# A 2-D spectral filter with backward pass: chunked complex column transform, and a twice-folded real one through DRAM

## The chip, the cores and the metric

The kernel runs on one core of one Trainium2 chip. Time is in device microseconds (us) of that core for one launch; lower is better. Times are medians of several runs; one execution was also taken with the hardware profiler. The engines are TensorE (PE, with its weight loads PEld), VectorE (DVE), ScalarE (ACT), GpSimd (POOL) and SyncE (SP). SP and POOL issue nearly all DMAs here.

## The reference

Two branches are mixed by a gate, and the kernel computes the output and all gradients. Branch A is a 2-D real Fourier transform of x (2048 x 1024), a product with a complex weight W (2048 x 513), and the transform back; branch B is a dense layer with squared relu and hidden width F = 3584.

```python
def _A_ref(x, w_r, w_i):
    X = rfft2(x.astype(float32), axes=(-2, -1))
    X = X * (w_r + 1j * w_i)
    return irfft2(X, s=(S, D), axes=(-2, -1)).astype(bfloat16)

def _B_ref(x, w1, b1, w2, b2):
    h = einsum("bsd,df->bsf", x, w1) + b1
    r = where(h > 0, h, 0)
    return einsum("bsf,fd->bsd", r * r, w2) + b2

g = sigmoid((x * gate_w).sum(-1, keepdims=True))
a = _A_ref(x, A_w_r, A_w_i)
b = _B_ref(x, B_w1, B_b1, B_w2, B_b2)
out = g * a + (1 - g) * b
```

Both branches work on x. The nine outputs are out, the gradients of x, w_r and w_i, of w1, b1, w2, b2 and of gate_w. The backward pass of branch A is the same transform on g times the incoming gradient, a product with the conjugate of W, and a transform back; the gradient of W is the product of the one spectrum with the conjugate of the other.

## The kernel before

Rows are taken as 16 tiles of 128; tile t holds the rows p*16 + t. P is 128, S = 2048, D = 1024, Df = 513.

*Loading (L266 to L293).* Each of the 16 tiles of x and of the incoming gradient is loaded, alternately by SP and POOL (`dma`, L186, takes the two queues in turn), transposed by TensorE in eight 128 x 128 blocks into xT and goT, and the gate sums are formed.

*Chunks (from L416).* The 520 padded columns of the half spectrum are cut in nine chunks of 64 (the last of 8). For each, `f1_stage` (matmul L325) multiplies the rows by cosine and sine matrices; `fwd_chain` (L348 to L377) does the transform over the 2048 rows as 128 times 16, both complex: matmuls with `amat`, transposes, matmuls with `kmat`. W is loaded by columns and transposed too (L467). `cmul` (L490 to L502) forms the three complex products, shared between DVE and POOL: the filtered spectrum `ybuf`, the backward one `dxb`, and the gradient of W, which goes to DRAM as gWc_scr. `inv_c_t` (L391 to L407) applies the 16-point stage backwards and transposes into the large buffer RT.

*Loops back.* `t_loop` (L540 to L590) runs over 16 tiles: matmuls with `apmat`, eight or nine transposes (L568), matmuls with the inverse row matrix g5 (L578), a scaled copy to `abf`, and a store to a_scr. The nine chunks of `dxb` come back from dX_scr through `inv_c_t` into the same RT, and `t_loop` runs again and stores to gx_scr. In the first run a dot product with the incoming gradient is formed (L590).

*Dense part.* goT is scaled by 1 - g (L621 to L626). Four row blocks of 512 rows (L677 to L806) run forward and backward through the dense layer and write out and gx. Then seven groups of hidden units (L849 to L868) give the gradients of w1 and w2: each has 128 matmuls at L858 from go and h2l, and 128 at L866 from dhl and x. In the third group the gradient of W is gathered from gWc_scr into `gall` by nine POOL DMAs (L849) and written to the outputs by two (L851, L852).

The order on each engine is the program's order; tiles with a tag share a ring of `bufs` buffers, and a DMA or operation that writes a tile waits until the last user of that buffer is done.

Of the kernel before, what the change touches and what calls it, by code (L numbers as in the profile page):

```python
# [10 lines left out]
P = 128  # L11
# [10 lines left out]
class Geo:  # L22

    def __init__(self, S, D, F, CC=64):
# [4 lines left out]
        self.L_LO = P // self.S2  # L29
        self.Df = D // 2 + 1  # L30
        self.NLH = -(-self.Df // self.L_LO)
        self.NCOLC = self.NLH * self.L_LO
        self.CC = CC
        assert CC % self.L_LO == 0
        self.CH = CC // self.L_LO
        self.chunks = []
        lh = 0
        while lh < self.NLH:
            n = min(self.CH, self.NLH - lh)
            self.chunks.append((lh, n))  # L40
            lh += n
        self.NJ = len(self.chunks)
        self.zbase = []
        b = 0
        for (lh0, n) in self.chunks:
            self.zbase.append(b)
            b += 2 * n * self.L_LO
        self.ZC = b
        self.NBZ = -(-self.ZC // P)
# [12 lines left out]

    def ccj(self, j):
        return self.chunks[j][1] * self.L_LO


def build_consts(g: Geo):
    S, D, S2, L_LO = g.S, g.D, g.S2, g.L_LO
    two_pi = 2.0 * np.pi
    c = {}  # L70
    c["identb"] = np.eye(P, dtype=np.float32).astype(ml_dtypes.bfloat16)
    c["ident16"] = np.eye(P, dtype=np.float32).astype(FDT_NP)
    CDS = np.zeros((g.NJ, P, g.DC, 2 * g.CC), dtype=np.float64)
    d = np.arange(D)
    for j, (lh0, n) in enumerate(g.chunks):
        CCj = n * L_LO
        ls = np.arange(lh0 * L_LO, lh0 * L_LO + CCj)
        ang = two_pi * ((ls[None, :] * d[:, None]) % D) / D
        cr = np.cos(ang)
        ci = -np.sin(ang)  # L80
        valid = (ls < g.Df)[None, :]
        cr = np.where(valid, cr, 0.0)
        ci = np.where(valid, ci, 0.0)
        ci[:, (ls % (D // 2)) == 0] = 0.0
        blk = np.concatenate([cr, ci], axis=1)
        CDS[j, :, :, : 2 * CCj] = blk.reshape(g.DC, P, 2 * CCj).transpose(1, 0, 2)
    c["cds"] = CDS.astype(np.float32).astype(ml_dtypes.bfloat16)
    pp = np.arange(P)[:, None]
    ff = np.arange(P)[None, :]
    A = np.zeros((P, S2, 3, P))  # L90
    Ap = np.zeros((P, S2, 3, P))
    for t in range(S2):
        m = (ff * (S2 * pp + t)) % S
        th = two_pi * m / S
        A[:, t, 0, :] = np.cos(th)
        A[:, t, 1, :] = -np.sin(th)
        A[:, t, 2, :] = np.sin(th)
        m2 = (pp * (S2 * ff + t)) % S
        ph = two_pi * m2 / S
        Ap[:, t, 0, :] = np.cos(ph)  # L100
        Ap[:, t, 1, :] = np.sin(ph)
        Ap[:, t, 2, :] = -np.sin(ph)
    c["amat"] = A.reshape(P, S2 * 3, P).astype(np.float32).astype(FDT_NP)
    c["apmat"] = Ap.reshape(P, S2 * 3, P).astype(np.float32).astype(FDT_NP)
    pt = np.arange(P) // L_LO
    pa = np.arange(P) % L_LO
    delta = (pa[:, None] == pa[None, :]).astype(np.float64)
    ang = two_pi * ((pt[:, None] * pt[None, :]) % S2) / S2
    K = np.zeros((P, 3, P))
    K[:, 0, :] = np.cos(ang) * delta  # L110
    K[:, 1, :] = -np.sin(ang) * delta
    K[:, 2, :] = np.sin(ang) * delta
    c["kmat"] = K.astype(np.float32).astype(FDT_NP)
    G = np.zeros((g.NBZ * P, D))
    for j, (lh0, n) in enumerate(g.chunks):
        CCj = n * L_LO
        ls = np.arange(lh0 * L_LO, lh0 * L_LO + CCj)
        ang = two_pi * ((ls[:, None] * d[None, :]) % D) / D
        coef = np.where((ls == 0) | (ls == D // 2), 1.0, 2.0)[:, None]
        valid = (ls < g.Df)[:, None]  # L120
        gr = np.where(valid, coef * np.cos(ang), 0.0)
        gi = np.where(valid, -coef * np.sin(ang), 0.0)
        gi[(ls % (D // 2)) == 0, :] = 0.0
        b = g.zbase[j]
        G[b : b + CCj] = gr
        G[b + CCj : b + 2 * CCj] = gi
    c["g5"] = G.reshape(g.NBZ, P, D).transpose(1, 0, 2).astype(np.float32).astype(FDT_NP)
    return c

# [14 lines left out]
def kernel(  # L144
# [30 lines left out]
    S2, L_LO, DC, DW, DCH, FC = g.S2, g.L_LO, g.DC, g.DW, g.DCH, g.FC  # L175
    CH, CC, NJ = g.CH, g.CC, g.NJ
# [6 lines left out]
    dmat_rr = _RR([nc.scalar])  # L183
# [4 lines left out]
    def dma_t(out, in_):  # L188
        return dmat_rr().dma_start_transpose(out=out, in_=in_)

    w_rv = A_w_r.rearrange("(k2 k1) l -> k1 k2 l", k1=P)
    w_iv = A_w_i.rearrange("(k2 k1) l -> k1 k2 l", k1=P)
    o2v = out_2.rearrange("(k2 k1) l -> k1 k2 l", k1=P)
    o3v = out_3.rearrange("(k2 k1) l -> k1 k2 l", k1=P)
# [10 lines left out]
    ident16 = pers.tile([P, P], FDT, name="ident16", tag="ident16")  # L205
    dma(ident16[:], cten["ident16"].ap())
    kmat = pers.tile([P, 3, P], FDT, name="kmat", tag="kmat")
    dma(kmat[:], cten["kmat"].ap())

# [8 lines left out]
    omg = pers.tile([P, S2], FP32, name="omg", tag="omg")  # L218
    gpg = pers.tile([P, S2], FP32, name="gpg", tag="gpg")
    rsx = pers.tile([P, S2], FP32, name="rsx", tag="rsx")  # L220
    rsgo = pers.tile([P, S2], FP32, name="rsgo", tag="rsgo")
# [8 lines left out]
    ones_f = pers.tile([P, 1], FP32, name="ones_f", tag="ones_f")  # L230
    nc.vector.memset(ones_f[:], 1.0)
    b2row = pers.tile([1, D], BF16, name="b2row", tag="b2row")
    dma(b2row[:], B_b2.rearrange("(o d) -> o d", o=1))
    dcval = pers.tile([1, 1], FP32, name="dcval", tag="dcval")
# [8 lines left out]
    a_scr = dram.tile([S2, P, D], BF16, name="a_scr")  # L243
    gx_scr = dram.tile([S2, P, D], BF16, name="gx_scr")
    dX_scr = dram.tile([NJ, P, 2 * CH * P], FDT, name="dX_scr")
    SC = S // P
    gWc_scr = dram.tile([NJ, P, 2, S2, CC], BF16, name="gWc_scr")
# [5 lines left out]
    with tc.tile_pool(name="p0sb", bufs=3) as p0, tc.tile_pool(  # L253
        name="p0ps", bufs=2, space=bass.MemoryType.PSUM
    ) as p0ps, tc.tile_pool(name="p0small", bufs=2) as p0s:
        sgate = p0s.tile([P, S2], FP32, name="sgate", tag="sgate", bufs=1)
        for which in range(2):
            src = x_perm if which == 0 else go_perm
            dstT = xT if which == 0 else goT
            for t in range(S2):  # L260
                xt = p0.tile([P, D], BF16, name="xt", tag="xt", bufs=8)
                dma(xt[:], src[t])
                junk = p0.tile([P, D], BF16, name="junk", tag="junk")
                junk2a = p0.tile([P, D], BF16, name="junk2a", tag="junk2a")
                if which == 0:
                    nc.vector.tensor_tensor_reduce(  # L266
                        out=junk[:], in0=xt[:], in1=gatew_bc[:], scale=1.0, scalar=0.0,
                        op0=ALU.mult, op1=ALU.add, accum_out=sgate[:, t : t + 1],
                    )
                    nc.scalar.activation(junk2a[:], xt[:], ACT.Copy, accum_out=rsx[:, t : t + 1])  # L270
                else:
                    nc.scalar.activation(junk2a[:], xt[:], ACT.Copy, accum_out=rsgo[:, t : t + 1])
                for dc0 in range(0, DC, 4):
                    nb = min(4, DC - dc0)
                    pt = p0ps.tile([P, 4, P], BF16, name="pt", tag="pt")
                    for i in range(nb):
                        nc.tensor.transpose(pt[:, i, :], xt[:, (dc0 + i) * P : (dc0 + i + 1) * P], identb[:])
                    nc.any.tensor_copy(out=dstT[:, dc0 : dc0 + nb, t * P : (t + 1) * P], in_=pt[:, 0:nb, :])
        nc.scalar.activation(gcol[:], sgate[:], ACT.Sigmoid)
        nc.vector.tensor_scalar(out=omg[:], in0=gcol[:], scalar1=-1.0, scalar2=1.0, op0=ALU.mult, op1=ALU.add)  # L280
        nc.vector.tensor_tensor(out=gpg[:], in0=gcol[:], in1=omg[:], op=ALU.mult)
        t1 = p0s.tile([P, 2], FP32, name="t1", tag="t1")
        nc.vector.reduce_sum(out=t1[:, 0:1], in_=rsx[:], axis=mybir.AxisListType.X)
# [644 lines left out]
```

## Time and profile before

| | us |
|---|---|
| median of three runs | 2336.31 |
| the runs | 2332.72, 2336.31, 2339.97 |
| span of the profiled execution | 2334.1 |
| loading and transposing | 0 to 75 |
| nine chunks | 75 to 465 |
| loops back | 465 to 749 |
| four row blocks | 749 to 1866 |
| weight gradients | 1866 to 2334 |

No other time of the profiled execution itself is listed than its span. The stages follow each other on TensorE, so their ends can be read from the lines of its instructions. In the views that follow, "busy" is the time in which an engine works on an instruction; "x" stands for the count; the granted clock is the share of full speed that TensorE was given in that stretch; "<-" after a number of idle microseconds names what ended the wait. A group's row has the busy time in us and the mean of one instruction in ns.

### The profile page before, as it was taken

The page shows a single profiled execution, that of the slowest core. Times are in us where ns is not written, and L with a number is a line of the kernel's source. Part 1 is how long each engine was busy: PE and PEld are TensorE (multiplying, and loading weights), DVE is VectorE, ACT ScalarE, POOL GpSimd, SP SyncE. Part 2 cuts the span into 40 slices and gives each one's busy share as a digit, 9 for nine tenths or more (in the row PEclk, how much of TensorE's full clock was granted, in tenths as well). Part 3 has the DMA queues.
Part 4 walks back from the last instruction along what each step waited for, and adds up shares of the span by engine and source line. Part 5 has one row for each costly group of instructions (what it writes and reads, how often), then busy time and mean ns, then how long its engine had stood idle before and what let it go on. Part 6 is the DMA issues. An engine that isn't in the chain of part 4 may idle for free. (4 is left out here: it accounts for less than half of the span.)

```text
span 2334.1 us, 29795 instructions
## 1 busy us (share of the span) xinstructions
PE 1920.0 (82%) x11632; PEld 965.5 (41%) x11632; DVE 555.9 (24%) x1114; ACT 723.1 (31%) x1550; POOL 558.9 (24%) x844
## 2 busy tenths in 40 slices
PE   2878878668788888888988799878977783999998
PEld 2756656523333344344433344324433231444443
DVE  4253453624323422223211222202202100000000
ACT  5756556423533343123410043103440010111111
POOL 2042232311011412242211221222121251222200
PEclk9988988679999899999999999999988987999999
DMA  5211110142212556575544455534573498333310
GB/s 156 87 38 37 51 42 24 38 119 77 74 42 74 179 189 215 176 207 164 205 138 145 125 192 191 166 120 158 165 248 124 131 259 136 112 109 112 109 39 26
DMA packets 198068, 291.61 MB, mean 125 GB/s; under 512 B 56743, under 2 KB 142661, under 8 KB 197670
## 3 DMA queue, kind: packets, MB, share of 16 engines
q0 software_dynamic: 48704, 151.04, 21.6%
q1 hardware_dynamic: 147926, 136.30, 18.8%
q10 hardware_dynamic: 1296, 2.36, 0.4%
q8 instruction: 91, 1.49, 0.3%
q14 instruction: 51, 0.42, 0.1%
HBM read 201.38 MB, written 88.23 MB: 124 GB/s over the span
## 5 line engine op out<-in xcount | busy, mean ns | idle before, releaser
L740 PE MATMUL acc<-w2c,h2T 128*128 128x512 bf16 x896 | 213.8, 393 | 48.7 <-DMA w2c<-in_B_w_dram 38.8
L704 PE MATMUL ph<-xT,w1g 128*128 128x512 bf16 x896 | 236.5, 387 | 7.2 <-DMA w1g<-in_B_w_dram 7.2
L858 PE MATMUL pw<-go,h2l 128*128 128x512 bf16 x896 | 204.9, 391 | 44.5 <-ACT wo L860 20.5
L797 PE MATMUL accg<-w1Ttc,dhT 128*128 128x512 bf16 x672 | 173.5, 398 | 58.6 <-DMA w1Ttc<-w1T_scr 49.8
L866 PE MATMUL pw<-dhl,x 128*128 128x512 bf16 x896 | 195.1, 379 | 3.9 <-ACT wo L868 3.9
L797 PEld LDWEIGHTS <-dhT 128*128 128x128 bf16 x896 | 87.1, 100 | 182.7 <-issue 106.2
L712 PE MATMUL pd<-goT,w2Tfc 128*128 128x512 bf16 x672 | 161.3, 381 | 0.2
L722 ACT COPY h2S<-ptr 128x512 bf16<-128x512 bf16 x112 | 65.6, 586 | 307.6 <-PE ptr L720 220.7
L740 PEld LDWEIGHTS <-h2T 128*128 128x128 bf16 x896 | 89.7, 101 | 168.5 <-issue 75.9
L858 PEld LDWEIGHTS <-h2l 128*128 128x128 bf16 x896 | 89.2, 100 | 159.0 <-issue 54.8
L578 PE MATMUL pa<-g,zT 128*128 128x512 f16 (+1 forms) x576 | 139.9, 381 | 0.0
L866 PEld LDWEIGHTS <-x 128*128 128x128 bf16 x896 | 87.5, 98 | 110.3 <-issue 5.0
L713 DVE SCALAR_TENSOR_TENSOR dhT<-pd,rT 128x512 bf16<-128x512 f32 x112 | 77.4, 691 | 207.9 <-PE pd L712 203.6
L860 ACT CAST wo<-pw 128x512 bf16<-128x512 f32 x56 | 32.7, 586 | 268.3 <-PE pw L858 150.5
L708 ACT ACTIVATE rT<-ph,b1col 128x512 bf16<-128x512 f32 x112 | 77.1, 688 | 124.2 <-PE ph L704 124.1
L704 PEld LDWEIGHTS <-w1g 128*128 128x128 bf16 x896 | 80.0, 99 | 66.5 <-DMA w1g<-in_B_w_dram 7.4
L878 DVE CAST r<-pb 1x512 bf16<-1x512 f32 x2 | 1.4, 678 | 444.7 <-PE pb L876 444.7
L712 PEld LDWEIGHTS <-w2Tfc 128*128 128x128 bf16 x672 | 65.8, 98 | 81.0 <-issue 3.8
L709 ACT ACTIVATE h2T<-rT 128x512 bf16<-128x512 bf16 x112 | 70.5, 629 | 90.4 <-PE acc L740 79.7
L868 ACT CAST wo<-pw 128x512 bf16<-128x512 f32 x56 | 32.8, 586 | 186.9 <-PE pw L866 135.2
L578 PEld LDWEIGHTS <-zT 128*128 128x128 f16 (+1 forms) x576 | 50.7, 97 | 87.7 <-issue 36.3
L186 POOL DMA_DIRECT2D out_dram<-wo x56 | 30.5, 545 | 228.4 <-ACT wo L860 114.7
(226 smaller groups left out, 2928.7 us busy)
## 6 DMA issues: line engine op xcount, KB each, us to landing
w1g<-in_B_w_dram SPq DMA_DIRECT2D x14, 1024.0 KB, 5.5
w1g<-in_B_w_dram POOLq DMA_DIRECT2D x14, 1024.0 KB, 6.1
w2c<-in_B_w_dram SPq DMA_DIRECT2D x28, 512.0 KB, 3.5
w2c<-in_B_w_dram POOLq DMA_DIRECT2D x28, 512.0 KB, 4.2
w2Tfc<-w2T_scr POOLq DMA_DIRECT2D x42, 256.0 KB, 3.6
w2Tfc<-w2T_scr SPq DMA_DIRECT2D x42, 256.0 KB, 2.8
w1Ttc<-w1T_scr POOLq DMA_DIRECT2D x84, 128.0 KB, 2.3
w1Ttc<-w1T_scr SPq DMA_DIRECT2D x84, 128.0 KB, 2.1
```

The costliest lines, as they stand in the source:

```text
L578: nc.tensor.matmul(pa[:, dch * DW : (dch + 1) * DW], lhsT=zT[0:w, blk, :], rhs=g5[0:w, blk, dch * DW : (dch + 1) * DW], start=(blk == 0), ...
L704: nc.tensor.matmul(ph[:], lhsT=w1g[:, dc, fcg * P : (fcg + 1) * P], rhs=xT[:, dc, cols], start=(dc == 0), stop=(dc == DC - 1))
L708: nc.scalar.activation(rT[:], ph[:], ACT.Relu, bias=b1col[:, fc : fc + 1])
L709: nc.scalar.activation(h2T[:, fc, :], rT[:], ACT.Square)
L712: nc.tensor.matmul(pd[:], lhsT=w2Tf[:, ec, :], rhs=dbT[:, ec, cols], start=(ec == 0), stop=(ec == DC - 1))
L713: nc.vector.scalar_tensor_tensor(out=dhT[:, fc, :], in0=pd[:], scalar=2.0, in1=rT[:], op0=ALU.mult, op1=ALU.mult, accum_out=gb1part[:, fc, ...
L722: nc.scalar.copy(out=stg[:, :, fcg * P : (fcg + 1) * P], in_=ptr[:])
L740: nc.tensor.matmul(accs[i][:], lhsT=h2T[:, fc, i * P : (i + 1) * P], rhs=w2c[:, r_, :], start=(fc == 0), stop=False)
L797: nc.tensor.matmul(accs[i][:], lhsT=dhT[:, fc, i * P : (i + 1) * P], rhs=w1Tt[:], start=(fc == 0), stop=(fc == FC - 1))
L858: nc.tensor.matmul(pw[:], lhsT=h2l[sc][:, fb * P : (fb + 1) * P], rhs=db_t[sc][:, ecols], start=(sc == 0), stop=(sc == SC - 1))
L866: nc.tensor.matmul(pw[:], lhsT=x_t2[sc][:, db * P : (db + 1) * P], rhs=dhl[sc][:], start=(sc == 0), stop=(sc == SC - 1))
L868: nc.any.tensor_copy(out=wo[:], in_=pw[:])
```

## The change

The transform of branch A is written anew; the dense part stays.

*Forward rows.* The complex row transform becomes a real one of half the width twice over: the row of 1024 is folded at 512 and at 256 (sum and difference of mirrored halves) on DVE, so four groups of 256 numbers remain. A real 16-point stage over the rows comes first, as eight matmuls with the data as weights and `kf` as the moving matrix, which at the same time transposes; for the second tensor `kf` is scaled by the gate. Eight matmuls with `cf` (2305 columns in all) give 1024 real numbers a row, even and odd frequencies, which are copied as u and stored to z_scr. Loading and transposing the tile for the dense part (`load_row`) is part of the same pass.

*Columns.* In eight steps m, two of the 16 column groups, m and 16 - m, are loaded from z_scr. `spectrum` unpacks them with sums and differences, and multiplies by `amat`; W and its gradient are read and written in their natural row order, so the transposes of W and of its gradient, gWc_scr and `gall` are gone. The products run on DVE; `inverse` multiplies by `apmat` and packs into y_scr.

*Back rows.* Each of 32 passes loads a row tile r, does the 16-point stage with `ki`, eight matmuls with `ci`, unfolds on DVE into yo and stores it to a_scr or gx_scr, now in f16 and unscaled. The scale YS is applied where the dense part uses them.

```diff
-            f1_stage("A", pair, [uv for (_, uv) in uA], jps, xT, None, cdsp)
-            f1_stage("B", pair, [uv for (_, uv) in uB], jps, goT, gcol, cdsp)
-            XSA, bufUA, bufTA = fwd_chain("A", j, jb, jps, bUA, uAv)
-            XSB, bufUB, bufTB = fwd_chain("B", j, jb, jps, bUB, uBv)
...
-        t_loop("B", RT, tb, tps, apmat, g5, gx_scr, False)
...
+        ps2 = fx.enter_context(tc.tile_pool(name="fps2", bufs=3, space=bass.MemoryType.PSUM))
...
+        def s1(T, i, xt, kmat):
+            uv = fb.tile([P, 2, H], FDT, name="uv", tag="uv", bufs=2)
+            nc.vector.tensor_tensor(out=uv[:, 0, :], in0=xt[:, 0:H], in1=xt[:, H:D], op=ALU.add)
+            nc.vector.tensor_tensor(out=uv[:, 1, :], in0=xt[:, 0:H], in1=xt[:, H:D], op=ALU.subtract)
...
+            nc.vector.tensor_tensor(out=f[:, 0:2, 1:Q], in0=a0, in1=a1, op=ALU.add)
+            nc.vector.tensor_tensor(out=f[:, 2:4, 1:Q], in0=a0, in1=a1, op=ALU.subtract)
...
+            for b in range(8):
+                nc.tensor.matmul(pk[:, b, :], lhsT=fl[:, b * P : (b + 1) * P], rhs=kmat, start=True, stop=True)
+            ft = fb.tile([P, 8, P], FDT, name="ft", tag="ft", bufs=2)
+            nc.scalar.copy(out=ft[:], in_=pk[:])
+            pu = ps2.tile([P, 2, H], FP32, name="pu", tag="ps2")
+            o = 0
+            for (b, bank, lo, n, st) in FWD:
+                nc.tensor.matmul(
+                    pu[:, bank, lo : lo + n], lhsT=ft[:, b, :], rhs=cf[:, o : o + n],
...
+            u = fb.tile([P, H, 2], FDT, name="u", tag="u", bufs=3)
+            nc.any.tensor_copy(out=u[:].rearrange("p j b -> p b j"), in_=pu[:])
+            dma(z_scr[T][:].rearrange("c (p i) l -> i (c p) l", i=S2)[i], u[:].rearrange("p j b -> p (j b)"))
...
+        def load_row(i, T):
+            xt = fb.tile([P, D], BF16, name=f"nat{T}", tag=f"nat{T}", bufs=2)
+            dma(xt[:], (go_perm if T else x_perm)[i])
+            pt = ps2.tile([P, DC, P], BF16, name="pt", tag="ps2")
+            for b in range(DC):
+                nc.tensor.transpose(pt[:, b, :], xt[:, b * P : (b + 1) * P], identb[:])
+            nc.scalar.copy(out=(goT if T else xT)[:, :, i * P : (i + 1) * P], in_=pt[:])
+            return xt
...
+                nc.vector.tensor_tensor(out=pm[:, 2:0:-1, :], in0=R, in1=I, op=ALU.add)
+                nc.vector.tensor_tensor(out=pm[:, 0::3, :], in0=R, in1=I, op=ALU.subtract)
...
+                mm(px[:, 0, :], lhsT=C, rhs=re, start=True, stop=False)
+                mm(px[:, 1, :], lhsT=C, rhs=im, start=True, stop=False)
...
+                mm(px[:, 0, :], lhsT=Sn, rhs=im, start=False, stop=True)
+                mm(px[:, 1, :], lhsT=N, rhs=re, start=False, stop=True)
+                (nc.scalar.copy if (j + T) % 2 == 0 else nc.vector.tensor_copy)(out=x[:, j, :, 0:H], in_=px[:])
+            nc.vector.tensor_tensor(out=x[:, :, :, 0::H], in0=sp[:], in1=sgn[:], op=ALU.mult)
...
+                (nc.scalar.copy if (j + T) % 2 == 0 else nc.vector.tensor_copy)(out=v[:, j, :, 0:H], in_=pv[:])
...
+            dma(y_scr[T][:].rearrange("c p l -> p c l")[:, m : m + 9 : 8, :], pc[:].rearrange("p j c l -> p j (c l)"))
...
+                V(out=t1_[:, :, :, 0:W1], in0=X, in1=wr, op=ALU.mult)
+                V(out=t2_[:, :, :, 0:W1], in0=X, in1=wi, op=ALU.mult)
...
+            for c_, dst_w in enumerate((out_2, out_3)):
+                nc.gpsimd.dma_start(out=rows2(dst_w, m), in_=gw[:, :, c_, 0:W1])
...
+                r = fb.tile([P, H, 2], FDT, name="r", tag="u", bufs=3)
+                nc.sync.dma_start(out=r[:].rearrange("p j b -> p (j b)"), in_=y_scr[T][:].rearrange("c (p i) l -> i (c p) l", i=S2)[i])
...
+                nc.scalar.copy(out=rt[:], in_=pk[:])
...
+                nc.scalar.copy(out=e[:], in_=pu[:])
...
+                yo = fb.tile([P, D], FDT, name="yo", tag="u", bufs=3)
...
+                dma((a_scr if T == 0 else gx_scr)[i], yo[:])
...
-                        out=ot[:], in0=a_pc[:], scalar=gcol[:, t : t + 1], in1=bsc[:], op0=ALU.mult, op1=ALU.add,
+                        out=ot[:], in0=a_pc[:], scalar=gcs[:, t : t + 1], in1=bsc[:], op0=ALU.mult, op1=ALU.add,
...
-                    nc.vector.tensor_tensor(out=gxo[:], in0=gx1[:], in1=gxf_pc[:], op=ALU.add)
+                    nc.vector.scalar_tensor_tensor(
+                        out=gxo[:], in0=gxf_pc[:], scalar=YS, in1=gx1[:], op0=ALU.mult, op1=ALU.add,
...
-            if fg == min(2, g.FG - 1):
...
-                            nc.gpsimd.dma_start(out=gall[:, :, :, j * CC : j * CC + CCj_], in_=gWc_scr[j][:, :, :, 0:CCj_])
-                    with nc.allow_non_contiguous_dma(reason="gw output rows"):
-                        nc.gpsimd.dma_start(out=o2v[:, :, :], in_=gall[:, 0, :, 0 : g.Df])
-                        nc.gpsimd.dma_start(out=o3v[:, :, :], in_=gall[:, 1, :, 0 : g.Df])
```

How the rows stand on three engines is shown below; the number behind a name tells apart the tiles of one name, each row is an instruction (line, operation, out<-in, size).

SP in the loop back of the first tensor, before: the loads for the next stage, then the stores, with no load between them.

```order
L186 DMA dX_scr_106<-dxb_4725 128x2048
L186 DMA dxl_6734<-dX_scr_106 128x2048
L186 DMA dxl_6812<-dX_scr_106 128x2048
L186 DMA a_scr_104<-abf_5865 128x1024
L186 DMA a_scr_104<-abf_5922 128x1024
```

SP in the back rows of the first tensor, now.

```order
L427 DMA r_2686<-y_scr0_100 128x1024
L427 DMA r_2722<-y_scr0_100 128x1024
L171 DMA a_scr_96<-yo_2713 128x1024
L427 DMA r_2758<-y_scr0_100 128x1024
L171 DMA a_scr_96<-yo_2749 128x1024
L427 DMA r_2794<-y_scr0_100 128x1024
L171 DMA a_scr_96<-yo_2785 128x1024
```

Loads and stores now alternate on one queue; r_2758 lies in the buffer of yo_2713, and r_2794 in that of yo_2749.

DVE in a chunk, before: products and sums of the complex multiplication with evictions of the next stage among them (POOL has other products).

```order
L490 TENSOR_TENSOR tmp2_5101<-xsb_A_4928,WS_5079 128x1024
L496 TENSOR_TENSOR ybuf_5102<-tmp1_5100,tmp2_5101 128x1024
L490 TENSOR_TENSOR tmp2_5101<-xsb_A_4928,WS_5079 128x1024
L352 CAST bufT_A_5514<-pA_5539 128x2x8
L502 TENSOR_TENSOR ybuf_5102<-tmp1_5100,tmp2_5101 128x1024
L490 TENSOR_TENSOR tmp2_5101<-xsb_B_5062,WS_5079 128x1024
L396 CAST rsb_a_5146<-pCi_5151 128x512
L496 TENSOR_TENSOR dxb_5103<-tmp1_5100,tmp2_5101 128x1024
```

DVE in a column step, now: the last two sums of the first tensor's filtered spectrum, the unpacking of the next step (pm), and then the second tensor's products.

```order
L403 TENSOR_TENSOR y_2193<-t1_2189,t2_2190 128x2x513
L404 TENSOR_TENSOR y_2193<-t1_2189,t2_2190 128x2x513
L319 TENSOR_TENSOR pm_2274<-z_2272 128x2x512
L347 TENSOR_TENSOR x1_2166<-sp_2167,k_sgn_125 128x4x2
L320 TENSOR_TENSOR pm_2274<-z_2272 128x2x512
L368 CAST v_2196<-si_2197 128x4
L399 TENSOR_TENSOR t1_2223<-x1_2166,w_2130 128x4x513
L367 CAST v_2196<-pv_2207 128x2x512
L400 TENSOR_TENSOR t2_2224<-x1_2166,w_2130 128x4x513
L371 TENSOR_TENSOR pc_2217<-v_2196 128x1024
```

A row has twice the elements, all products are here, and evictions (L367) stand between them.

ACT in the forward rows, now: of a pass the copy of the transposed tile, of the 16-point stage (ft), and of the wide matmuls (u).

```order
L272 CAST u_403<-pu_394 128x2x512
L286 COPY xT_65<-pt_408 128x8x128
L262 CAST ft_438<-pk_429 128x1024
L297 ACTIVATE gcol_69<-sgate_106 128x1
L272 CAST u_449<-pu_440 128x2x512
L286 COPY goT_66<-pt_456 128x8x128
L262 CAST ft_483<-pk_474 128x1024
```

Three copies of 1024 columns a pass all stand on ACT, and each lies between two groups of TensorE's matmuls.

More of the change, by code (lines that the diff above doesn't have):

```diff
@@ L75, in build_consts @@
[L75 to L86, printed above, removed]
@@ L114, in build_consts @@
[L114 to L126, printed above, removed]
@@ L251 @@
     dh_scr = dram.tile([g.FG, SC, P, g.FGW], BF16, name="dh_scr")
[L253 to L279, printed above, removed]
@@ L578, in t_loop @@
                     nc.tensor.matmul(
-                        pa[:, dch * DW : (dch + 1) * DW], lhsT=zT[0:w, blk, :], rhs=g5[0:w, blk, dch * DW : (dch + 1) * DW],
-                        start=(blk == 0), stop=(blk == g.NBZ - 1),
-                    )
-            abf = tb.tile([P, D], BF16, name="abf", tag="abf")
-            for dch in range(DCH):
-                nc.scalar.activation(abf[:, dch * DW : (dch + 1) * DW], pa[:, dch * DW : (dch + 1) * DW], ACT.Copy, scale=inv_sd)
-            dma(dst_scr[t], abf[:])
@@ new lines @@
+                dma((a_scr if T == 0 else gx_scr)[i], yo[:])
+                if T == 0:
+                    go_ = fb.tile([P, D], BF16, name="go_", tag="nat1", bufs=2)
+                    dma(go_[:], go_perm[i])
+                    junk = fb.tile([P, D], BF16, name="junkt", tag="f", bufs=2)
+                    nc.vector.tensor_tensor_reduce(
+                        out=junk[:], in0=yo[:], in1=go_[:], scale=YS, scalar=0.0,
+                        op0=ALU.mult, op1=ALU.add, accum_out=aGo[:, i : i + 1],
+                    )
```

624 lines of the change are left out of this document (232 added, 392 removed).

## The prediction

> **What bounds the kernel now.** I read the page's head first, then busy time by stage, the chain that ended last, and single stretches.
>
> ```profile
> span 2334.1 us, 29795 instructions
> ...
> PE 1920.0 (82%) x11632; PEld 965.5 (41%) x11632; DVE 555.9 (24%) x1114; ACT 723.1 (31%) x1550; POOL 558.9 (24%) x844
> ```
>
> TensorE (PE) works 82% of 2334.1 us. The median of the runs shown, 2336.31, lies 2.2 above this span; what lies around the span is put at that, and the sum is made in the span. By stage, with the columns length, busy us (count) of PE, weight load, DVE, ACT and POOL, granted clock, DMA share, GB/s:
>
> ```profile
> 0.00:75.00 75.00, 29.65 (x260) 23.11 (x261) 41.09 (x94) 44.00 (x80) 17.14 (x29) 0.95 0.56 160
> 75.00:465.00 390.00, 308.34 (x3285) 236.57 (x3286) 170.51 (x243) 223.14 (x665) 113.53 (x76) 0.85 0.14 40
> 465.00:749.00 284.00, 228.25 (x1257) 98.33 (x1256) 82.53 (x138) 106.52 (x238) 41.28 (x95) 0.95 0.23 71
> 749.00:1866.00 1117.00, 941.77 (x4976) 425.34 (x4974) 257.23 (x633) 283.87 (x456) 279.82 (x466) 0.96 0.54 171
> 1866.00:2334.00 468.00, 412.00 (x1857) 182.16 (x1857) 4.54 (x9) 65.53 (x112) 107.09 (x179) 0.94 0.43 113
> ```
>
> The rows are loading and transposing, the nine chunks, the loops back, the four row blocks, and the weight gradients. The first three, 749 us, are the transform: TensorE is busy 566 of them. The last two are the dense layers, which the change leaves alone but for two scalings and one gather. The chain that ended last shows that gather (start, length, what):
>
> ```profile
> 1926.33 7.76 DMA gall<-gWc_scr
> 1935.94 26.81 DMA out_dram<-wo
> 1963.43 18.32 DMA out_dram<-wo
> 1982.49 22.83 PE pw L858 x96
> 2005.33 27.63 PE pw L866 x128
> ```
>
> **The change, part by part.** *End of the transform.* The dense part's first loads stand on SP behind the last gx_scr store:
>
> ```profile
> 748.86 0.32 SPq L186 DMA_DIRECT2D gx_scr<-abf  x1
> 751.01 0.33 SPq L186 DMA_DIRECT2D w2r<-in_B_w_dram  x1
> ```
>
> So the transform ends at 751.0. I build its new end from the engine that is late in each of three stages.
>
> *Forward rows (32 passes).* Start: 4.2 MB of constants go ahead of the second row's load on SP, and the first pass waits for b1row as now.
>
> ```profile
> 8.49 0.20 PE L240 MATMUL b1ps<-identb,b1row 28*128 28x28 bf16 x1 [8.49 <-DMA b1row<-in_B_b_dram]
> amat<-c_amat SPq DMA_DIRECT2D x1, 1536.0 KB, 6.2
> xt<-in_grad_out_dram SPq DMA_DIRECT2D x8, 256.0 KB, 3.9
> ```
>
> 4.2 MB at 1536 KB per 6.2 us is 17 us; 8.7 + 17 + 3.9 = 29.6, and pass 3 reaches its wide matmuls near 31.5.
>
> A pass on TensorE is eight transposes, eight 128-column products, then eight matmuls of 2305 columns in all. Each group waits for ACT to copy the one before, and the next pass's transposes stand behind the last. So the wide matmuls and three ACT copies of 1024 columns add up, less the part where the next transposes run beside the u copy, since PSUM has three buffers.
>
> ```profile
> L573 ACT COPY zT<-pzt 128x1024 f16<-128x1024 f16 x17 | 17.2, 1012 | 4.5 <-PE pzt L568 4.5
> 603.50 0.62 PE L403 MATMUL pTi<-ident,rsb 128*128 128x128 f16 x8
> 144.94 1.04 PE L515 MATMUL pWo<-identb,gW 128*128 128x128 bf16 x8 [6.45 <-DVE gW L496]
> 600.00:620.00 20.00, 14.41 (x101) 1.00 0.28 93
> 130.00:150.00 20.00, 10.88 (x73) 0.67 0.14 40
> ```
>
> Eight 128-column matmuls took 0.62 us where the granted clock was 1.00 (fourth row) and 1.04 where it was 0.67 (fifth). Taking off 0.17 us for the tail (an estimate), a column is 0.44 or 0.85 ns, and 2305 columns 1.18 or 2.13 us. ACT gives 3 x 1.01; handovers I estimate at 0.1. A pass is 4.3 us at the full clock and 5.3 at the low one. ACT then sets the pace with TensorE in gaps of a microsecond, so I take 4.45, near the full clock. 31.5 + 28 x 4.45 + 1.2 + 1.0 = 158. DVE needs at most 3.6 us a pass and is hidden.
>
> z goes out and back through DRAM at 2.3 and 3.2 us:
>
> ```profile
> gx_scr<-abf POOLq DMA_DIRECT2D x8, 256.0 KB, 2.3
> dxl<-dX_scr SPq DMA_DIRECT2D x4, 512.0 KB, 3.2
> ```
>
> The first tensor's last row is out 4.4 us earlier, so DVE begins the columns at 160.
>
> *Columns (8 steps).* DVE does nearly all of it:
>
> ```profile
> L496 DVE TENSOR_TENSOR ybuf<-tmp,tmp 128x1024 f16<-128x1024 f16 x8 | 5.5, 692 | 0.8
> L496 DVE TENSOR_TENSOR ybuf<-tmp,tmp 128x128 f16<-128x128 f16 x1 | 0.2, 225 | 0.1
> L492 DVE SCALAR_TENSOR_TENSOR tmp<-xsb_B,xsb_A 128x1024 f16<-128x1024 f16 x32 | 37.8, 1221 | 0.5
> L766 DVE TENSOR_TENSOR dg<-aGo,dg 128x1 f32<-128x1 f32 x16 | 2.2, 156 | 0.0
> L396 DVE CAST rsb<-pCi 128x512 f16<-128x512 f32 x10 | 6.9, 688 | 30.3 <-PE pCi L392 29.9 <-PE pCi L395 0.3
> ```
>
> A two-byte tensor_tensor costs 0.521 ns an element (692 less 225 ns over 896): 1.23 us for 2052. An f32 eviction of 1024 I take as 1.22, twice the 688 less its fixed 0.15, or as the third row. Per tensor and step: two folds 1.38, eviction 1.22, edges 0.16, two products 2.46, two sums 1.39, eviction 1.22, edge 0.14, unfolding 1.38 + 0.31 = 9.67. Both tensors and the weight gradient (two products, two sums, an edge: 4.01) make 23.35 us; eight, less some 4 us in step 0, which folds nothing, make 183. The stalls where DVE waits for the inverse matmuls and ACT's eviction are shown nowhere in this form: 1.0 us a step if TensorE has the full clock, 4.6 if the low one (estimates from the column prices above). I take 3, since TensorE mostly idles here: 24, and 3 for filling. 160 + 183 + 27 = 370. Before, POOL shared the products and DVE had 171 us of work in 390.
>
> The gradient's 16 output DMAs leave from POOL, which has nothing behind them in this stage but y stores of alternate tensors; these I cost at nothing, covered by the next step's 23 us.
>
> *Back rows (32 passes).* The tile r that a row is loaded into and the tile yo that the finished row is stored from share three buffers, taken in turn: r of pass i+2 gets the buffer of yo of pass i, so its load waits until that store has landed. A period of two passes is thus a circle: DVE 1.95 (five operations at the prices above), store, load, eight products, ACT copy, wide matmuls, ACT copy.
>
> ```profile
> a_scr<-abf SPq DMA_DIRECT2D x16, 256.0 KB, 2.0
> w2Tfc<-w2T_scr SPq DMA_DIRECT2D x42, 256.0 KB, 2.8
> ```
>
> 1.95 + 2.0 + 2.8 + 0.65 + 1.04 + 1.18 + 1.04, and handovers of some 0.25: 10.9 us; 12.3 at the low clock. I take 11.6, in the middle. First row at 372; 15 periods, 174; pass 31 some 4 us behind pass 30: 550, and with DVE and store **554**, 197 us before 751.0. In the first tensor's passes a dot product also runs,
>
> ```profile
> L590 DVE CUSTOM_DVE_ANT_0 junkt<-abf,got 128x1024 bf16<-128x1024 bf16 x16 | 19.5, 1217 | 0.0
> ```
>
> hidden in the 5 us that DVE waits per pass; uncovered it costs 16 x 1.2 = 19 us.
>
> *Dense part.* The row blocks keep their work and order; loads swap between SP and POOL, which I put at nothing, from -5 to +5. Two scale factors move into operations of the same length.
>
> *Gather gone.*
>
> ```profile
> 1908.59 10.52 PE L866 MATMUL pw<-dhl,x 128*128 128x512 bf16 x48
> 1936.50 1.16 POOL L852 DMA_DIRECT2D out_dram<-gall  x1
> 1961.68 0.54 POOL L186 DMA_DIRECT2D dhl<-dh_scr  x1 [20.60 <-DMA out_dram<-gall]
> 1963.46 6.54 PE L858 MATMUL pw<-go,h2l 128*128 128x512 bf16 x16 [19.14 <-ACT wo L868]
> ```
>
> From 1908.59 to 2005.33 stand two groups of 128 matmuls that take 27.63 each in the chain: 96.7 - 55.3 = 41 us lost. POOL waits 20.60 us for the gathered output before it can issue dhl. All of it should go; I take 40, since some DMA traffic remains.
>
> Sum: 2334.1 - 197 - 40 = 2097, plus 2.2: **2099 us**.
>
> **Rivals.** (1) *TensorE stays at the low clock through the transform.* For it: TensorE idles in small gaps throughout, and the row at 0.67 has 10.88 us busy in 20. Against: the stage from 465 shows 0.95 at 80% busy. Forward rows 28 x 0.8 = 23, columns 8 x 1.6 = 13, back rows 15 x 0.7 = 11: 2146. [...]
>
> (2) *The gap at 1940 stays.* The wo stores that hold the chain may be held by the h2l and dhl loads, not by the gather: + 40, 2140. Against it speaks POOL's wait on out_dram<-gall.
>
> (3) *DVE does not halve products with W.* W is bf16, spread over two planes, against f16. No such row is in the trace; bounds are the 692 and 1221 rows. At the latter a product costs 1.06 us more: six a step, + 51; with all sums and folds at 0.53 more, fourteen a step, + 110: 2150 to 2210. [...]
>
> (4) *The shared buffers do not bind.* If loads were early enough, a back pass would cost about 3.55 us (two ACT copies, wide matmuls, handovers): 32 x 3.55 = 114 instead of 182, so 2032. Against it: three buffers, two users.
>
> (5) *Slower.* The circle's round trip through DRAM is the one cost that can grow large:
>
> ```profile
> 1866.00:1908.00 42.00, 32.54 (x127) 0.84 0.95 272
> go<-in_grad_out_dram SPq DMA_DIRECT2D x8, 256.0 KB, 12.5
> ```
>
> At a DMA share of 0.95 a load of 256 KB took 12.5 us. Store and load at that price are 25 us in place of 4.8, so 16 x 20 = 323: 2422, slower. It decides from 237 / 16 = 14.8 us more a period. But two rows out and two in per 11.6 us are only some 90 GB/s, plus go rows, far below 272.
>
> **How the numbers follow.** Forecast 0.56, (1) 0.15, (2) 0.12, (3) 0.08, (4) 0.06, (5) 0.03. The forecast's own range: all at the full clock -32, DVE and row blocks -5 to -12: 2055; upward the low clock in part and a round trip 1 us longer (+16): 2130. To (1) and (2) belongs the stretch up to 2155; outside remain (4), most of (3) and (5), under 0.2: **2045 to 2160**. A measurement of this kernel tells 0.3% from no change; (5) alone can be slower, 0.03, and its border 0.01 within 0.3%: faster 0.96.
>
> **What would show it.** Forward passes 4.3 to 4.6 us apart between wide matmuls, ending near 158; DVE busy over 85% from 160 to 370, products with W at 1.23 us; r loads each released by a yo store, 11 to 12 us per two; first w2r load near 554; the weight-gradient groups without a gap over 5 us. I am wrong if forward passes overlap or stretch (a fourth ACT job on the path), if products take 2.3 us, if r loads start before the store lands, or if the gap in the last stage returns at another store.

## The result, and the profile after

The changed kernel took 2091.47 us (median of four runs, 2083.98 to 2101.05) against 2335.4 for the one before, run beside it: a ratio of 0.896, with a 95% interval of 0.8932 to 0.8989. The profiled execution has a span of 2089.6 us. Forecast were 2099 us, with 2045 to 2160 as the range.

The page's head of the changed kernel, against that of before:

```profile
span 2089.6 us, 23144 instructions
...
PE 1642.3 (79%) x8586; PEld 772.8 (37%) x8586; DVE 566.9 (27%) x1272; ACT 564.1 (27%) x786; POOL 447.5 (21%) x784
```

TensorE lost 278 us of work and the span 244.5. The busy times by stage, with the same columns as before; the stages are now forward rows, columns, back rows, row blocks and weight gradients:

```profile
0.00:167.00 167.00, 93.74 (x780) 71.84 (x781) 70.46 (x181) 104.29 (x115) 37.20 (x104) 0.82 0.42 143
167.00:343.00 176.00, 102.28 (x485) 38.44 (x483) 163.17 (x256) 47.81 (x42) 15.81 (x23) 0.70 0.41 134
343.00:543.00 200.00, 93.61 (x502) 55.84 (x500) 73.24 (x203) 64.52 (x72) 13.18 (x24) 0.53 0.32 103
543.00:1660.00 1117.00, 940.21 (x4950) 423.62 (x4951) 251.53 (x618) 281.69 (x448) 287.91 (x459) 0.96 0.53 171
1660.00:2089.00 429.00, 412.47 (x1876) 183.08 (x1873) 8.53 (x15) 65.74 (x112) 93.43 (x175) 0.98 0.32 106
```

The row blocks take 1117 us in both kernels. Everything that was gained lies in the transform, 749 us before and 543 now, and in the weight gradients, 468 before and 429 now. In the columns DVE is busy 163 of 176 us. In the back rows no engine is busy half the time, and TensorE has a granted clock of 0.53.

The waits in the back rows (who waited for what, us in total, times, longest) show the circle:

```profile
DVE tt L445 <- ACT e L443: 113.7, 30, 6.7
...
PEld L431 <- DMA r<-y_scr: 77.7, 25, 6.2
ACT rt L433 <- PE pki L431: 67.4, 21, 6.0
PE pki L431 <- DMA r<-y_scr: 67.0, 21, 5.9
```

DVE waits for ACT, ACT for TensorE, TensorE for the load of r. SP's own timeline shows what the load waits for:

```profile
438.56 0.32 SPq L171 DMA_DIRECT2D a_scr<-yo  x1
440.97 0.32 SPq L427 DMA_DIRECT2D r<-y_scr  x1
447.22 0.32 SPq L171 DMA_DIRECT2D gx_scr<-yo  x1
449.28 0.32 SPq L427 DMA_DIRECT2D r<-y_scr  x1
```

The loads shown are issued 2.1 and 2.4 us after a store of yo (2.1 to 3.7 us over the first tensor's passes), and such a store takes 2.0 us to land. What the loads of r waited for on SP's queue between 345 and 540 us:

```profile
SPq L427 <- DMA gx_scr<-yo: 55.7, 14, 8.7
SPq L427 <- DMA a_scr<-yo: 31.7, 16, 3.3
```

The DMA list of the changed kernel has the median times to landing:

```profile
z_scr<-u POOLq DMA_DIRECT2D x32, 256.0 KB, 2.7
z<-z_scr SPq DMA_DIRECT2D x16, 512.0 KB, 3.8
r<-y_scr SPq DMA_DIRECT2D x32, 256.0 KB, 3.0
...
a_scr<-yo SPq DMA_DIRECT2D x16, 256.0 KB, 2.0
```

### The profile page after: what moved, and what is told of

Read it like the earlier page. It is cut to its first block, busy times and chain, and to the rows that moved or that the text cites. A ratio compares the mean times of both kernels' runs of the same rounds, so it can differ in the third digit from the quotient of the medians.

```text
span 2089.6 us, 23144 instructions
## 1 busy us (share of the span) xinstructions
PE 1642.3 (79%) x8586; PEld 772.8 (37%) x8586; DVE 566.9 (27%) x1272; ACT 564.1 (27%) x786; POOL 447.5 (21%) x784
## 5 line engine op out<-in xcount | busy, mean ns | idle before, releaser
L697 ACT CAST wo<-pw 128x512 bf16<-128x512 f32 x56 | 32.9, 587 | 253.1 <-PE pw L695 240.6
L266 PE MATMUL pu<-k_cf,ft 128*128 128x256 f16 (+3 forms) x256 | 48.8, 347 | 59.9 <-ACT ft L262 59.9
L437 PE MATMUL pui<-k_ci,rt 128*128 128x256 f16 (+3 forms) x256 | 63.7, 425 | 37.5 <-ACT rt L433 37.5
L597 DVE SCALAR_TENSOR_TENSOR ot<-a_pc,gcs,bsc 128x512 bf16<-128x512 f16 x32 | 23.8, 750 | 242.6 <-ACT bsc L595 236.5
```

The costliest lines, as they stand in the source:

```text
L437: nc.tensor.matmul(pu[:, bank, lo : lo + n], lhsT=rt[:, b, :], rhs=ci[:, o : o + n], start=bool(st & 1), stop=bool(st & 2), skip_group_che ...
```

## The experiments

All of them start from the changed kernel, but for the seventh. Back rows are compared from the first unfolding on DVE to the last (343.80 to 539.18 in the changed kernel, 195.4 us; a period of two passes there is 12.3 us over passes 0 to 30, and 12.2 over passes 4 to 30, the stretch for which the periods of the experiments are given). Where one run was made, its total is given with "once". The median of the kernel before moved between 2326.7 and 2336.2 us from one set of runs to another, so the readings rest on the stages in the traces, and totals of four runs are given as ratios.

**1. Buffers of its own for yo.**

```diff
-                yo = fb.tile([P, D], FDT, name="yo", tag="u", bufs=3)
+                yo = fb.tile([P, D], FDT, name="yo", tag="z", bufs=3)
```

> The changed kernel with one tag changed: yo of the back rows lies in the three buffers of z, so r and yo no longer share. If the shared ring sets the back rows (two passes per round trip through DRAM, 12.4 us in the changed kernel's trace), a pass falls to its chain on ScalarE and TensorE, 3.4 us at the full clock and 4.1 at the low one: the stage goes from 200 us to 107 to 131, the total to 2000 to 2025. If DRAM bandwidth or the matmul-copy chain sets it, the stage stays above 185 us and the total within 15 us of 2091.

Measured: 1991.97 us, ratio 0.8546 (0.8515 to 0.8577). The back rows took 101.6 us, a pass 3.24, a little under the 107 to 131 and the 3.4 expected. The window of that stage:

```profile
345.00:445.00 100.00, 50.53 (x488) 38.11 (x486) 68.58 (x186) 58.80 (x61) 11.38 (x21) 0.99 0.60 194
```

The same work moves at 194 GB/s instead of 103, so bandwidth did not bind, and the clock is 0.99, which nobody asked for. Two things changed at once: the load no longer waits, and TensorE is no longer at a clock of 0.53. The next runs take them apart.

**2. Extra matmuls to keep the clock up, first try.** Four matmuls of 512 columns behind each 16-point stage, shown here, and twelve behind the wide ones of odd passes, with constants only.

```diff
                 nc.scalar.copy(out=rt[:], in_=pk[:])
+                dm2 = ps1.tile([P, 512], FP32, name="dm2", tag="sp")
+                for _ in range(4):
+                    nc.tensor.matmul(dm2[:], lhsT=ki[:], rhs=ci[:, 0:512], start=True, stop=True, skip_group_check=True)
```

> The changed kernel with extra matmuls in the back rows whose results nobody reads: four of 512 columns behind each 16-point stage and twelve behind the wide matmuls of every odd pass, where TensorE waits for r. They delay work by at most a few tenths of a us if the clock is full. If the low clock costs 1.4 us a period of two passes (1.03 instead of 0.61, and 2.11 instead of 1.17), and activity raises it, the period falls from 12.4 to 11.0 and the stage by 22 us. If the clock is not what the period hangs on, or is not raised by this, the stage stays at 200 us or gets longer by up to 2 us a period.

Measured: 2083.44 us once, and the back rows 200.4 us. A miss, since the scheduler put nearly all the extra matmuls, which depend on no row, among the first tensor's passes. Two windows of TensorE alone (busy us and count, clock, DMA share, GB/s):

```profile
350.00:420.00 70.00, 69.20 (x408) 1.00 0.36 113
425.00:535.00 110.00, 54.34 (x298) 0.56 0.28 93
```

In the first tensor's passes TensorE was full and two passes took 14.2 us; in the second's there was no extra work and the clock was 0.56.

**3. The extra matmuls held in place.** They use the pass's own tiles as weights, so they can't run ahead. The lines taken out here are those of the second run.

```diff
-                    nc.tensor.matmul(dm2[:], lhsT=ki[:], rhs=ci[:, 0:512], start=True, stop=True, skip_group_check=True)
+                    nc.tensor.matmul(dm2[:], lhsT=r[:, 0:P, 0], rhs=ci[:, 0:512], start=True, stop=True, skip_group_check=True)
...
-                        nc.tensor.matmul(dmy[:], lhsT=ki[:], rhs=ci[:, 0:512], start=True, stop=True, skip_group_check=True)
+                        nc.tensor.matmul(dmy[:], lhsT=rt[:, 7, :], rhs=ci[:, 0:512], start=True, stop=True, skip_group_check=True)
```

> The changed kernel with the shared ring kept, and the extra matmuls of the first try held in their place by using the pass's own tiles as weights: four of 512 columns behind each 16-point stage, twelve behind the wide matmuls of odd passes; nobody reads their results. If the low clock is part of the ring's period, the granted clock of the stage rises from 0.54 and the period of two passes falls from 12.4 us to about 11.0, the stage by 15 to 22 us. If the period is memory alone, it stays at 12.4 whatever the clock. If the extra work is in the way, it rises above 12.4.

Measured: 2074.78 us once. Window of the stage:

```profile
345.00:523.00 178.00, 126.84 (x777) 66.40 (x775) 66.85 (x180) 59.77 (x61) 11.39 (x21) 0.93 0.35 110
```

The clock rose from 0.53 to 0.93 and the stage fell from 195.4 to 182.1 us, 13 less, a little under the 15 to 22 expected. From pass 4 to pass 30 a period was 11.4 us instead of 12.2. So the low clock is a part of the period, some 0.8 us, and the small part.

**4. Four buffers instead of three, one number.** r and yo still take turns, but r of pass i+2 now comes into the buffer of r of pass i.

```diff
-                r = fb.tile([P, H, 2], FDT, name="r", tag="u", bufs=3)
+                r = fb.tile([P, H, 2], FDT, name="r", tag="u", bufs=4)
...
-                yo = fb.tile([P, D], FDT, name="yo", tag="u", bufs=3)
+                yo = fb.tile([P, D], FDT, name="yo", tag="u", bufs=4)
```

> The changed kernel with one number changed, the buffers of the tag that r and yo share, from three to four (room for it from one buffer less for kg and from sgate lying in dsc). r and yo still take turns, but with an even number r of pass i+2 gets the buffer of r of pass i, not that of yo. If the parity of the ring is the cause, a back pass falls to 3.24 us as with buffers of its own, and the stage from 195 to about 102 us between its first and last unfolding. If r and yo are too few buffers altogether, one more helps by a part only, and a pass stays above 4.5 us.

Measured: 2050.09 us once; stage 159.4 us, a period of two passes 10.3 us. The parity was a part of the cause, not the whole: 1.9 us left the period, about what the store takes to land (2.0), and the rest stayed, so that a pass is still above 4.5 us. SP's rows in the timeline suggest why, and below them is all that its queue waited for between 345 and 500 us:

```profile
402.66 0.32 SPq L171 DMA_DIRECT2D a_scr<-yo  x1
...
403.07 0.38 SPq L427 DMA_DIRECT2D r<-y_scr  x1
...
408.73 0.32 SPq L171 DMA_DIRECT2D a_scr<-yo  x1
...
409.14 0.38 SPq L427 DMA_DIRECT2D r<-y_scr  x1
```

```profile
SPq L171 <- DVE yo L451: 132.4, 23, 9.2
```

The load is issued 0.4 us behind the store, no longer 2.1. No load of r waits for anything of its own there; it stands behind a store on SP's queue, and the store waits for DVE to finish yo. If that is what holds the loads back, the order on SP, with two loads ahead of the first store, is a second circle; the next two runs test it.

**5. and 6. The stores on POOL, with four buffers and with three.**

```diff
-                dma((a_scr if T == 0 else gx_scr)[i], yo[:])
+                nc.gpsimd.dma_start(out=(a_scr if T == 0 else gx_scr)[i], in_=yo[:])
...
-                    dma(go_[:], go_perm[i])
+                    nc.gpsimd.dma_start(out=go_[:], in_=go_perm[i])
```

> The ring of four, and the stores of yo and the loads of go_ all on POOL, so that SP holds only the loads of r in the back rows. If what was left of the period with four buffers (10.3 us for two passes) is that a load of r stands on SP behind a store that waits for VectorE, a pass falls to the chain of matmuls and copies, 3.24 us, and the stage to about 102 us. If the round trip is still in the buffers, or POOL's stores are late, a pass stays above 4.5 us.

> The changed kernel's ring of three, with the stores of yo and the loads of go_ all on POOL. If the shared buffer alone is enough to hold the load back until the store has landed, the period of two passes stays at 12.0 to 13.0 us, POOL's stores taking 0.3 us longer to land than SP's. If SP's order was the whole cause, a pass falls to 3.24 us.

Measured: with four buffers 1991.67 us once, stage 103.1 us, a pass 3.24; with three 2083.87 us once, stage 195.9 us, a period 12.6. The four kernels make a square:

| back rows, us (period of two passes) | stores as in the change | all stores on POOL |
|---|---|---|
| ring of three | 195.4 (12.2) | 195.9 (12.6) |
| ring of four | 159.4 (10.3) | 103.1 (6.5) |

Opening the queue alone gives nothing, the buffer alone 36 us, both 92. These gains include the clock, which was 0.53 in both kernels with three buffers, 0.61 with four, and 0.93 with both circles open. Buffers of its own for yo (the first run) opened both: SP's timeline there has five loads ahead of the first store, where the changed kernel has two, so a store no longer stood in front of the next load that was needed.

**7. The kernel before without its gather, and without the two writes of what it gathers.**

```diff
-            if fg == min(2, g.FG - 1):
-                with tc.tile_pool(name="gwout", bufs=1) as gwo:
...
-                        nc.gpsimd.dma_start(out=o3v[:, :, :], in_=gall[:, 1, :, 0 : g.Df])
```

> The kernel before without the gather in the third group: gall and the two outputs written from it are left out, so the gradient of W isn't written. If the gather holds POOL and so the loads, the stage of weight gradients loses 41 us, 468 to 427, and the total falls to some 2290. If the loads of h2l and dhl or the wo stores make the gap by themselves, the stage loses less than 10 us.

Measured: 2292.56 us once beside 2336.17 with it, 43.6 less. The windows of the weight gradients with the gather stand in the prediction (468 us); without it:

```profile
1866.00:2290.00 424.00, 407.92 (x1865) 181.58 (x1864) 8.52 (x15) 65.52 (x112) 92.48 (x173) 0.98 0.32 107
```

**8. Evictions of the column steps on ScalarE.**

```diff
-                (nc.scalar.copy if (j + T) % 2 == 0 else nc.vector.tensor_copy)(out=x[:, j, :, 0:H], in_=px[:])
+                nc.scalar.copy(out=x[:, j, :, 0:H], in_=px[:])
...
-                (nc.scalar.copy if (j + T) % 2 == 0 else nc.vector.tensor_copy)(out=v[:, j, :, 0:H], in_=pv[:])
+                nc.scalar.copy(out=v[:, j, :, 0:H], in_=pv[:])
```

> The changed kernel with all spectrum and inverse evictions of the column steps on ScalarE, none on VectorE. If VectorE's work sets the column stage, each step loses four evictions of 1.14 us start to start, 4.6 us, in all 36 us: the stage falls from 175 us to some 140 to 150. If the path is eviction and inverse matmuls one after the other, VectorE waits for two ScalarE copies of 1.0 in a row and the stage stays within 10 us of 175.

Measured: 2050.72 us once. From ScalarE's first spectrum copy to the last edge of the weight gradient 168.3 to 314.6, 146 us, where the changed kernel has 166.2 to 342.4, 176. With its evictions gone VectorE's stage is 30 us shorter, so VectorE's work sets it.

**9. The transposed tiles copied on VectorE.**

```diff
-            nc.scalar.copy(out=(goT if T else xT)[:, :, i * P : (i + 1) * P], in_=pt[:])
+            nc.vector.tensor_copy(out=(goT if T else xT)[:, :, i * P : (i + 1) * P], in_=pt[:])
```

> The changed kernel with the copies of transposed tiles into xT and goT on VectorE instead of ScalarE. If ScalarE's three copies set a forward pass, a pass loses 0.9 us, 4.65 to 3.75, and the stage 29 us. If at the low clock the matmul groups set it (2.1 + 1.06 + 1.06 + one copy of 1.04 = 5.3, as in its slow passes), the stage loses under 10 us.

Measured: 2043.74 us once. The last u copy starts at 127.91 instead of 161.12, 33 us earlier; a pass takes 3.5 us in the stretch below (659 matmuls, 24 a pass, at a clock of 0.97). The same window of the changed kernel and of this one:

```profile
30.00:127.00 97.00, 57.00 (x501) 45.14 (x500) 46.92 (x118) 66.03 (x74) 22.25 (x63) 0.80 0.36 117
```

```profile
30.00:127.00 97.00, 58.76 (x659) 47.27 (x657) 73.36 (x177) 63.11 (x69) 30.89 (x84) 0.97 0.43 143
```

With ScalarE's third copy out of the way TensorE does 659 matmuls instead of 501 in the stretch, at a clock of 0.97 instead of 0.80. The copies leave TensorE waiting, and in the changed kernel the clock falls beside it: there a pass took 4.36 us where the clock was 1.00 (39.20 to 43.56) and 5.29 where it was 0.74 (75.38 to 80.67).

**10. u written without gaps.**

```diff
-            nc.any.tensor_copy(out=u[:].rearrange("p j b -> p b j"), in_=pu[:])
+            nc.any.tensor_copy(out=u[:], in_=pu[:].rearrange("p b j -> p j b"))
```

> The changed kernel with the interleaving of u made on the reading side: the copy writes u without gaps and reads the two PSUM banks in turn. If the scattered two-byte writes make the copy 1.30 us instead of 1.01 and the copy lies on the path, the copy goes to 1.01 and the forward rows lose 32 x 0.29 = 9 us. If reading with steps costs as much, the copy stays at 1.3 us or gets longer, and so does the stage.

Measured: 2081.35 us once. The last u copy starts at 152.48, 8.6 us earlier. The group of this copy before the edit and after it (busy, mean ns of one, idle):

```profile
L272 ACT CAST u<-pu 128x1024 f16<-128x1024 f32 x32 | 41.7, 1302 | 50.3 <-PE pu L266 50.3
```

```profile
L272 ACT CAST u<-pu 128x1024 f16<-128x1024 f32 x32 | 32.4, 1012 | 47.6 <-PE pu L266 47.6
```

Reading in turns costs no more than the other copies of this size (1012 ns, as at L443 of the changed kernel); writing every second element costs 0.29 us a copy.

**11. The first, eighth and ninth together,** and **12. the tenth added.**

> The changed kernel with the three single edits that shortened their stages put together: yo in the buffers of z, the transposed tiles copied on VectorE, the spectrum and inverse evictions on ScalarE. If the three stages are bound apart from each other, the gains add: back rows -96, forward rows -33, columns -29, total -158, ratio to the kernel before about 0.83. If one edit takes what another needs (VectorE in the forward rows, ScalarE in the columns), the sum falls short by over 15 us.

> The combined kernel with the interleaving of u made on the reading side too. If the u copy still lies on the path of a forward pass, 32 x 0.29 = 9 us go: the ratio to the kernel before falls from 0.829 to 0.825. If with the transposed tiles off ScalarE another chain sets the pass, under 3 us go.

Measured: 1934.07 us, ratio 0.8289 (0.8247 to 0.8331); and 1921.28 us, ratio 0.8258 (0.8236 to 0.8279). The dense part's first load, at 543.62 in the changed kernel, is at 385.83 and 377.57: 158 us earlier, the sum of the parts, and 8 more. The last is not told from the eleventh by the ratios, whose intervals overlap, only by the trace. Both are faster than the kernel before and than the changed one. The stages of the twelfth:

```profile
0.00:125.00 125.00, 71.40 (x776) 56.23 (x777) 86.66 (x213) 67.22 (x81) 41.22 (x104) 0.98 0.56 190
125.00:272.00 147.00, 87.89 (x489) 35.69 (x488) 128.98 (x224) 77.33 (x74) 17.11 (x24) 0.78 0.52 167
272.00:374.00 102.00, 50.48 (x495) 38.01 (x492) 70.98 (x193) 60.84 (x65) 11.42 (x21) 1.00 0.58 190
```

## Why the prediction was right, step by step

| step | forecast | measured |
|---|---|---|
| a forward pass, us | 4.45 | 4.66 |
| last u copied, at | 158 | 162.4 |
| VectorE begins the columns, at | 160 | 167.5 |
| columns, us | 210 | 175 |
| period of two back passes, us | 11.6 | 12.3 |
| last back pass behind the one ahead, us | 4 | 10.2 |
| dense part begins, at | 554 | 543.6 |
| weight gradients, less than before | 40 | 39 |

**Forward rows: the mechanism holds, two sizes were off.** ScalarE's three copies in a row with the wide matmuls set the pass (run 9). The copy of u was put at 1.01 us, from a copy whose writing had no gaps, and took 1.30 (run 10, 8.6 us for the stage). The clock moved between the two prices, as two passes show:

```profile
66.32 1.17 PE L266 MATMUL pu<-k_cf,ft 128*128 128x512 f16 x8 [2.30 <-ACT ft L262]
...
75.38 2.10 PE L266 MATMUL pu<-k_cf,ft 128*128 128x512 f16 x8 [1.48 <-ACT ft L262]
```

The forecast had TensorE "in gaps of a microsecond" and so near the full clock. That such gaps leave the clock near full was the author's estimate, which no row of the kernel before shows; the gaps were 1.5 to 2.3 us, and the clock 0.82 (in run 9, with 1.4 us idle a pass, 0.97). The 0.17 us taken off for a tail agrees with rows of the kernel before: in the weight gradients a matmul of 512 columns lasts 379 (L866) to 391 ns (L858), and 128 in a row take 27.63 us, 216 ns each, 0.16 to 0.18 us less. At a clock of 1.00 a pass took 4.36 us, close to the 4.3 counted, although the u copy was longer: ScalarE's copies begin some 0.1 us before the one ahead ends (they start at 156.35, 157.51 and 158.41 us in one pass, where the first two last 1.30 and 1.02). That the start was some 3 us earlier than forecast (wide matmuls of pass 3 at 28.6) gave part of it back. From the last u copy to VectorE's first operation it took 5.1 us, 3 more than the 2 forecast: the store took 2.7 us and the first load 3.4, where 2.3 and 3.2 were counted, and the first spectrum's matmuls, which hold VectorE until 167.5 after the load has landed at 164.2, had under 1 us in the sum.

**Columns: the mechanism holds, the term is 35 us too large.** The price of each operation was right: a product with W took 1227 ns where 1.23 us were counted, so that rival (3) is out. That a bf16 W beside f16 costs what two f16 tensors cost was the author's estimate, as the kernel before has no such row; the changed kernel takes 1234 ns for a product of two f16 tensors of this size (L409) and for the one with W:

```profile
L399 DVE TENSOR_TENSOR t<-x,w 128x2052 f16<-128x2052 f16 x16 | 19.6, 1227 | 0.1
```

What failed is that durations were added up as if each began at the end of the one before. VectorE's timeline in a column step:

```profile
220.85 1.22 DVE L399 TENSOR_TENSOR t<-x,w 128x2052 f16<-128x2052 f16 x1
221.98 1.22 DVE L367 CAST v<-pv 128x1024 f16<-128x1024 f32 x1
223.12 1.22 DVE L400 TENSOR_TENSOR t<-x,w 128x2052 f16<-128x2052 f16 x1
224.25 0.68 DVE L371 TENSOR_TENSOR pc<-v 128x1024 f16<-128x1024 f16 x1
224.85 0.69 DVE L373 TENSOR_TENSOR pc<-v 128x1024 f16<-128x1024 f16 x1
```

Starts lie 1.13 and 0.60 us apart where the operations last 1.22 and 0.68: each begins some 0.08 us before the last one ends. The 183 us of durations occupy only the 163 us that the window counts as busy: 20 of the 35. The other 15 are the stalls and the filling, put at 24 and 3 us, which were some 12 in all. The 24 put TensorE nearer its low clock because it mostly idles there, which was the author's estimate; the clock was 0.70.

**Back rows: the circle is right, but it is not the only one.** It was worked out at 10.9 us at the full clock and 12.3 at the low one, and taken in the middle at 11.6. It ran near the low clock (0.53) and took 12.3. So the choice of the middle was the term mis-sized, by 11 us in all. The clock's own price was put too high: held at a clock of 0.93 (run 3, with the extra matmuls) the circle took 11.4 us and not 10.9, and which part of it is longer no run singles out. Another 6 us came at the end, where the last pass stood 10.2 us behind the one ahead and not 4. In the second tensor's passes the stores leave by turns from SP and POOL, landing in 2.0 and 2.3 us, and the periods of the two turns were about 11.9 and 12.6 us, so the distance grew; that the store's queue is the cause isn't tested. What the prediction did not see is that SP's order would still have held the stage at 10.3 us a period with the buffers opened (run 4, against 6.5 in run 5). Rival (4), that the shared buffers don't bind, was wrong for this kernel, and its price, 3.55 us a pass, was close to the 3.24 of the runs without a circle.

**Rival (1), the low clock,** came true in the back rows, and in part in the columns (0.70) and the forward rows (0.82); in the back rows run 3 prices it at some 0.8 us a period, in the forward rows a mean pass of 4.66 against 4.36 makes it some 9 us, and in the columns no run prices it. In the back rows TensorE waited up to 5.9 us for r, at a clock of 0.53. The forward rows had no such wait, TensorE's longest between 35 and 160 us being 2.3 us, and the clock of that stretch was still only 0.83. In the back rows of the first run, where the matmuls' longest wait was 1.9 us, the clock was 0.99 with TensorE busy half the time. The two rows have the total, the times and the longest; what decides between them these runs do not show.

```profile
PE pu L266 <- ACT ft L262: 52.7, 27, 2.3
...
PE pui L437 <- ACT rt L433: 45.5, 28, 1.9
```

**Gather:** 39 us against 40; taken out of the kernel before, together with the writes of what it gathers, it gave 44 (run 7). Rival (2) is out. **Rival (5)** did not come: the loads took 3.0 us and the stores 2.0.

That the total came within 8 us of the forecast is partly luck: the columns' 35 us too many stand against 8 us too few at their start and 17 in the back rows (11 in the periods and 6 at the last pass). What the runs bear out is what bounds each stage, more than the sum.

## What to carry to other kernels

Before asking what engine bounds a load-compute-store loop, list for each buffer whose last use releases it, and for each queue what stands ahead of the load: here either alone closed a circle through DRAM, and only opening both freed the loop (195.4 to 103.1 us). An odd number of buffers (here three) shared by two tiles that take turns ties the load of one to the store of the other; an even number (here four) does not. When a stage is bound by one engine's operations, take their distance from start to start, not their durations (1.13 against 1.22 us on VectorE here), and see whether a neighbour that idles (ScalarE in the columns, VectorE in the forward rows) can take its plain copies (30 and 33 us here).

## What the runs showed of the hardware

An idle TensorE was not just idle: freed of its waits for r (up to 5.9 us), the same back rows ran at a granted clock of 0.99 instead of 0.53, so that the wide matmuls on the path shrank from 2.1 to 1.2 us as well, and extra matmuls that nobody reads made the stage shorter (195.4 to 182.1 us, at a clock of 0.93) while TensorE's busy time there rose from 91 to 127 us. A lowered clock came beside short waits too: in the forward rows, with none above 2.3 us between 35 and 160 us, the clock was 0.83, and with one copy less between the matmuls (run 9, 30 to 127 us) it was 0.97 instead of 0.80. A ScalarE copy from PSUM that writes every second two-byte element takes 1.30 us instead of 1.01, while reading PSUM in turns from its two banks takes the same 1.01 as a copy without steps.
